# One core, decode step with adaLN, cached attention and a Mish MLP: the last weights loaded in another order and in more, smaller transfers, and four matmuls on zeros taken out

## The chip, the cores and the metric

One core of one Trainium2 chip. The metric is the device time of one execution in microseconds; the time of a kernel is the median of its runs. TensorE is PE in the profile (PEld is its weight load), VectorE is DVE, ScalarE is ACT, GpSimd is POOL, SyncE is SP. A letter q behind an engine (SPq) means its sequencer: it issues transfers and waits.

## The reference

Two rows (batch 2, one token each) of width 512 go through one transformer block. All inputs are float32.

```
mod = silu(c) @ w_mod, cut in six: sa, ca, ga, sb, cb, gb       # 512 wide each
h = layernorm(x) * (1 + ca) + sa
q = h @ wq                                # 32 heads of 128
p = softmax(q . k_cache * 128**-0.5)      # 4096 keys in each of 2 x 32 heads
x = x + ga * ((p @ v_cache) @ wo)
h = layernorm(x) * (1 + cb) + sb
a = h @ w1 + b1                           # 1376 wide
a = a * tanh(softplus(a))                 # Mish
out = x + gb * (a @ w2)
```

The two caches hold 268 MB of the 297 MB that are read. Everything else is weights: `w_mod`, `wq`, `wo`, `w1`, `w2`.

## The kernel before

Three rooms in SBUF, each of 64 KB a partition, take all large data in turn. In the first part a room holds the keys of one head and the values of an earlier head (`pair`); VectorE multiplies keys by the query and sums along the head (lines 336 and 340), ScalarE takes the exponentials, TensorE multiplies by the values (line 382). The list `plan` holds the loads in order with what each has to wait for: a load is issued as soon as everything that was in its room has been used (`used`, `holds`). All large loads are issued by one queue, SP's, from one line, 69, in the helper `load`. Transfers start in the order in which they are issued; an engine that needs a piece waits for the semaphore of the transfer that brings it.

After the last keys the rooms are filled once more, in this order: `wo` (all but its last two heads); `two`, the values of two heads, in two transfers; `last`, the values of the last head in two transfers (3072 and 1024 KB); the rest of `wo` (512 KB); `w1` in two transfers (1376 KB each); and `tail`. `tail` takes the room of `two`, so its transfers are issued when TensorE has used both heads of it (`values(H - 2)`, line 486). It holds the last sixth of `w_mod`, called `mod5` (1024 KB, 8 KB a partition), and `w2`, cut in 11 chunks of 128 rows and 512 columns (`NCH`, 256 KB each, 2 KB a partition). It arrives in four transfers: `mod5` with chunks 0 to 4 (2304 KB), chunks 5 to 7 (768 KB), chunks 8 and 9 (512 KB), chunk 10 (256 KB).

The work behind the last values is one chain: attention output (line 491), the second layernorm folded into the first layer (lines 502 to 559), Mish on VectorE and ScalarE (lines 572 to 580, its result is `actt`), and the second layer `yps` (line 585), 88 matmuls: eight records for each chunk, four groups of columns, two passes. Between the first layer and the second TensorE computes the gate `gb` from `mod5` (`modulation`, line 241, 32 matmuls; ScalarE copies it out by `keep`), then runs `idle(4)`: four matmuls of a tile of zeros, `busy`, into a PSUM bank that nobody reads any more (line 260). At the end VectorE multiplies `yps` by the gate (line 593), adds the residual (line 594), and SP issues the transfer of the output (line 595). Each engine runs its instructions in program order.

Of the kernel before, what the change touches and what calls it, by code (L numbers as in the profile page):

```python
# [7 lines left out]

F32 = mybir.dt.float32
BF16 = mybir.dt.bfloat16  # L10
AF = mybir.ActivationFunctionType
ALU = mybir.AluOpType
AX = mybir.AxisListType
# [1 line left out]
P = 128  # L15
# [3 lines left out]
D = 512  # L19
# [9 lines left out]
ROOM = 2 * KV  # L29
ALONE = (8, 16)  # L30
WO_FIRST = H - 2


def behind(h):
# [10 lines left out]
def kernel(ctx: ExitStack, tc: tile.TileContext, src: dict, out: bass.AP):  # L45
    nc = tc.nc
# [6 lines left out]
    const = ctx.enter_context(tc.tile_pool(name="const", bufs=1))  # L53
# [4 lines left out]
    def room(n, name):  # L58
        return rooms.tile([P, ROOM], F32, tag=f"room{n}", name=name)
# [7 lines left out]
    def load(t, lo, ap):  # L67
        piece = t[:, lo : lo + ap.shape[1]]
        nc.sync.dma_start(out=piece, in_=ap)
        return piece  # L70
# [26 lines left out]
    def load_wo(n):  # L97
        late["wo"] = room(n, "wo")
        load(late["wo"], 0, src["wo"][:, : WO_FIRST * D])
        w_t["wo"] = late["wo"].rearrange("p (h n) -> p h n", h=H)  # L100
# [6 lines left out]
    def load_last(n):  # L107
# [5 lines left out]
        lo = KV  # L113
        load(late["wo"], WO_FIRST * D, src["wo"][:, WO_FIRST * D :])
        w_t["w1"] = t[:, lo : lo + G * F].rearrange("p (k n) -> p k n", k=G)
# [7 lines left out]
    def load_tail(n):  # L123
# [4 lines left out]
        for part in src["w2"]:  # L128
            load(t, lo, part)
            lo += part.shape[1]  # L130


    plan, holds = [], {0: [("w", "wq")], 1: [("w", "mod")], 2: [("k", 0)]}
    order = (1, 0, 2)
    for h in range(1, H):
        n = order[(h - 1) % 3]
        plan.append((lambda n=n, h=h: load_keys(h, n), n, list(holds[n])))
        holds[n] = [("k", h)] + ([] if h in ALONE else [("v", behind(h))])
    n = order[(H - 1) % 3]
    for what, items in (  # L140
# [6 lines left out]
        n = order[(order.index(n) + 1) % 3]  # L147
    n = next(r for r in holds if holds[r] is not None)
# [3 lines left out]
    def used(*items):  # L152
# [8 lines left out]
    rows = ident.rearrange("p (g r) -> p g r", g=G)  # L161
# [6 lines left out]
        out=fold, in_=ident.rearrange("p (g r) -> p r g", g=G), axis=AX.X, op=ALU.add  # L168
# [3 lines left out]
        out=mean_w, in0=fold[:, None, :].to_broadcast([P, G, R]), scalar1=1.0 / D, scalar2=None, op0=ALU.mult  # L172
# [11 lines left out]
    ct = const.tile([P, G, R], F32, name="ct")  # L184
    ht = const.tile([P, G, R], F32, name="ht")
    h2t = const.tile([P, G, R], F32, name="h2t")
    x2t = const.tile([P, G, R], F32, name="x2t")
    e_t = [[const.tile([P, NB, R], F32, name=f"e{i}_{b}") for b in range(B)] for i in range(4)]
    ot_last = const.tile([P, 2 * B], F32, name="ot_last")
    busy = const.tile([P, 512], BF16, name="busy")  # L190
    for t in (ct, ht, h2t, x2t, *(t for pair in e_t for t in pair), busy):
        nc.gpsimd.memset(t, 0.0)
    ov = [psum.tile([P, 512], F32, tag=f"ov{i}", name=f"ov{i}", bufs=1) for i in range(2)]

# [41 lines left out]
    def modulation(name, lo, n, t):  # L236
        ps = wide_ps(f"modps{name}")[:, : n * P].rearrange("p (m n) -> p m n", m=n)
        t = t[:, :, D * lo : D * (lo + n)]
        for k in range(G):
            for g in range(G):  # L240
                nc.tensor.matmul(  # L241
                    ps[R * g : R * (g + 1)],
                    lhsT=ct[:, k, :],
                    rhs=t[:, k, :].rearrange("p (m n) -> p m n", m=n)[:, :, P * g : P * (g + 1)],
                    start=(k == 0),
                    stop=(k == G - 1),
                )
        return ps
# [5 lines left out]

    def small(name):
        return const.tile([P, G, B], F32, name=name)

    def idle(n):
        for _ in range(n):
            nc.tensor.matmul(ov[1], lhsT=busy[:, 0:P], rhs=busy, start=True, stop=True)  # L260


    cps = small_ps("cps")[:, : 2 * G * B]
# [39 lines left out]
    for half in range(2):  # L303
        ps = wide_ps(f"qps{half}")
        for k in range(G):
            for g in range(G):
# [3 lines left out]
                    lhsT=ht[:, k, :],  # L310
                    rhs=w_t["wq"][:, k, 512 * c : 512 * (c + 1)],
                    start=(k == 0),
                    stop=(k == G - 1),
# [148 lines left out]
    for g in range(G):  # L462
        nc.tensor.matmul(  # L463
            xps[:, g], lhsT=late["att_sb"][:, P * g : P * (g + 1)], rhs=fold[:, 0:B],
            start=(g == 0), stop=False, skip_group_check=True,
# [23 lines left out]
    for i in range(2):  # L489
        for g in range(G):  # L490
            nc.tensor.matmul(
                xps[:, g],
                lhsT=w_t["wo"][:, H - 2 + i, P * g : P * (g + 1)],
                rhs=ot_last[:, B * i : B * (i + 1)],
                start=False,
                stop=(i == 1 and g == G - 1),
# [31 lines left out]
    for k in range(1, G):  # L528
# [5 lines left out]
        out=st[:, 2], in0=v_sum, scalar1=-0.5 / D, scalar2=-0.5 * EPS, op0=ALU.mult, op1=ALU.add  # L534
# [17 lines left out]
    lo = 0  # L552
    for g in reversed(range(G)):
# [3 lines left out]
        lo = hi  # L557
    for j in range(NJ):
        nc.tensor.matmul(
            fps[:, G * B * j : G * B * (j + 1)],  # L560
            lhsT=hq_pad[:, P * j : P * (j + 1)],
            rhs=coef,
            start=False,
            stop=(j == NJ - 1),
            skip_group_check=True,
        )
    x2_rows = keep("x2", x2ps)
    gps = modulation("5", 0, 1, w_t["mod5"])
    idle(4)
    f = const.tile([P, 3, NJ * G, B], F32, name="f")  # L570
    hid = fps.rearrange("p (n b) -> p n b", b=B)
    nc.vector.tensor_scalar(out=f[:, 0], in0=hid, scalar1=30.0, scalar2=None, op0=ALU.min)
# [10 lines left out]
    for n in range(NCH):  # L583
        for t in range(G):
            nc.tensor.matmul(  # L585
                yps[R * t : R * (t + 1), :P],
                lhsT=actt[:, n, :],
                rhs=w_t["w2"][:, n, P * t : P * (t + 1)],
                start=(n == 0),
                stop=(n == NCH - 1),  # L590
# [5 lines left out]
        out=out.rearrange("b o (g n) -> g (b o) n", n=P),  # L596
        in_=y[0 :: R // B, :],
# [3 lines left out]
def _lay_out(np, a):  # L601
    def rows(w):
        return w.reshape(-1, P, w.shape[-1]).transpose(1, 0, 2)

    def eight(v):
        return v.reshape(B, G, P).transpose(1, 0, 2).reshape(G * B, P)

    def head_rows(t, h):
        return t[:, h].reshape(B, P, NS * DH).transpose(1, 0, 2).reshape(P, KV)

    def join(*parts):
        return np.ascontiguousarray(np.concatenate([t.reshape(P, -1) for t in parts], axis=1))

    k, v = a["A_k_cache"], a["A_v_cache"]
    pair = np.stack([join(head_rows(k, h), head_rows(v, o)) for h, o in PAIRS])
    single = np.stack(
        [head_rows(k, h) for h in (0, *ALONE)] + [head_rows(v, h) for h in (H - 3, H - 2, H - 1)]
    )
    wm = rows(a["w_mod"])
    starts = np.cumsum((0,) + WIDTHS)  # L620
    b1c = np.zeros((P, NJ * G, B), a["B_b1"].dtype)
    w2 = np.zeros((P, NCH, D), a["B_w2"].dtype)
    for n, (g, j) in enumerate(CHUNKS):
        f0 = starts[g] + P * j
        f1 = min(f0 + P, starts[g + 1])
        b1c[: f1 - f0, n] = a["B_b1"][f0:f1, None]
        w2[: f1 - f0, n] = a["B_w2"][f0:f1]
    return {
        "cx": np.ascontiguousarray(np.concatenate([eight(a["c"]), eight(a["A_x"])])),
        "mod01234": join(wm[:, :, : 5 * D], b1c),  # L630
        "wq": join(rows(a["A_wq"])),
        "pair": pair,
        "single": single,
        "wo": join(rows(a["A_wo"])),
        "w2_0": join(wm[:, :, 5 * D :], w2[:, :5]),
        "w1": join(rows(a["B_w1"])),
        "w2_1": join(w2[:, 5:8]),
        "w2_2": join(w2[:, 8:10]),
        "w2_3": join(w2[:, 10:]),
    }  # L640


# [18 lines left out]
```

## Time and profile before

| | us |
|---|---|
| median of 3 runs (698.69 to 698.79) | 698.79 |
| the profiled execution, device time | 698.93 |
| its span in the profile | 697.2 |
| DVE busy in the span | 587.6 |
| PE busy in the span | 292.9 |
| mean DMA rate over the span, GB/s | 427 |

In the span, time 0 is the start of the program on the core and all times are counted from it. The profiled execution lies 0.14 us above the median. What the change touches lies in the last 25 us, from the issue of `tail` at 672.9 us on. A row of a timeline has the start, the duration, the engine, the line, the operation and the tiles, and how long the engine was idle before it and who released it. A row on transfers has their number, the size of one and the time from issue to landing, which is the moment the last of the DMA engines that carry it has reported.

### The profile page before, as it was taken

Reading aid. Unit: us, or ns where it says so; the run is one execution under the profiler, and the core shown is the slowest. Engines: PE = TensorE matmul, PEld = TensorE weight load, DVE = VectorE, ACT = ScalarE, POOL = GpSimd, SP = SyncE. Lnnn points to the kernel's source line nnn. Section 1 sums busy time; section 2 is a strip of 40 time slices with the busy share of each in tenths; the row PEclk is TensorE's granted clock in tenths of the full one; section 3 lists DMA queues with packets and bytes.
Section 4 is the critical chain, followed back from the end, with each engine's and each line's share of the span. In section 5 each row is a group of like instructions: output and inputs, shape, how many; then the busy total and the mean of one; then the engine's idle time right before and its main releaser. Section 6 shows DMA issues by size and latency. Waiting matters only on the chain.

```text
span 697.2 us, 4054 instructions
## 1 busy us (share of the span) xinstructions
PE 292.9 (42%) x1679; PEld 100.6 (14%) x1680; DVE 587.6 (84%) x240; ACT 39.5 (6%) x187; POOL 4.7 (1%) x22
## 2 busy tenths in 40 slices
PE   2360435432350435443504453444322453443886
PEld 1110101110110101111101111111100111110244
DVE  3039999999899999999999999999999899999102
ACT  1000000000000000000000000000000000000000
POOL 2000000000000000000000000000000000000000
PEclk9775565666655666566655558665765566556879
DMA  9999999999999999999999999999999999999996
GB/s 407 406 448 425 432 456 429 422 429 440 445 429 425 426 440 440 432 430 416 446 440 430 432 432 437 432 429 440 429 433 432 426 440 432 433 432 413 434 418 252
DMA packets 6686, 297.49 MB, mean 427 GB/s; under 512 B 756, under 2 KB 780, under 8 KB 1292
## 3 DMA queue, kind: packets, MB, share of 16 engines
q1 hardware_dynamic: 6636, 297.23, 98.8%
q8 instruction: 13, 0.21, 0.1%
q14 instruction: 5, 0.04, 0.0%
q10 hardware_dynamic: 32, 0.01, 0.0%
HBM read 297.23 MB, written 0.00 MB: 426 GB/s over the span
## 4 chain that ended last, share of the span: by engine, by line
DMA 49%; DVE 45%; PE 5%; issue 0%; ACT 0%; SPq 0%; DVEq 0%
DMA kv<-in_pair 40%; DVE kv L336 22%; DVE s L340 21%; DMA two<-in_single 4%; PE ov L382 2%; DMA tail<-in_w 2%; DMA first<-in_mod 2%; PE modps L241 1%; DVE n L358 1%; DVE n L357 1%; PE yps L585 0%; PE otp L398 0%; PE att L422 0%; PE last_ps L463 0%; DVE m L350 0%
## 5 line engine op out<-in xcount | busy, mean ns | idle before, releaser
L336 DVE TENSOR_TENSOR kv<-kv,qb 128x8192 f32<-128x8192 f32 x32 | 277.9, 8684 | 44.2 <-DMA kv<-in_pair 22.5
L340 DVE TENSOR_REDUCE s<-kv 128x64 f32<-128x8192 f32 x32 | 277.4, 8667 | 0.0
L382 PE MATMUL ov<-kv,e 128*32 128x512 f32 x928 | 168.6, 893 | 5.2 <-ACT e L366 5.2
L362 PE MATMUL mb<-n,ones 2*128 2x2 f32 x64 | 17.7, 344 | 221.4 <-DVE n L358 221.4
L321 PE MATMUL qb<-q_sb,row_of 32*128 32x512 f32 x32 | 28.4, 1035 | 65.4 <-DVE kv L336 65.4
L382 PEld LDWEIGHTS ov<-kv,e 128*32 128x32 f32 x928 | 36.9, 156 | 118.7 <-issue 109.6
L362 PEld LDWEIGHTS mb<-n,ones 2*128 2x128 f32 x64 | 15.8, 303 | 230.3 <-issue 155.5
L352 PE MATMUL mt<-ident,m 128*2 128x128 f32 x64 | 13.7, 300 | 75.8 <-DVE m L350 75.8
L363 ACT COPY m<-mb 128x2 f32<-128x2 f32 x32 | 5.1, 160 | 532.2 <-PE mb L362 423.7
L366 ACT ACTIVATE e<-s,m 128x32 f32<-128x32 f32 x64 | 20.0, 314 | 1.2
L321 PEld LDWEIGHTS qb<-q_sb,row_of 32*128 32x128 f32 x32 | 8.8, 302 | 73.7 <-DVE kv L336 67.8
L352 PEld LDWEIGHTS mt<-ident,m 128*2 128x2 f32 x64 | 3.1, 82 | 97.4 <-DVE m L350 76.7
L410 DVE RECIPROCAL total<-l 128x8 f32<-128x8 f32 (+1 forms) x9 | 1.7, 184 | 14.7 <-PE l L408 14.7
L308 PE MATMUL qps<-wq,ht 128*32 128x512 f32 x64 | 9.5, 761 | 10.5 <-DMA wq<-in_wq 10.5
L366 ACT ACTIVATION_READ_ACCUMULATOR e<-s,m 128x1 f32 x64 | 11.9, 186 | 0.0
L398 PE MATMUL otp<-pick,o 128*128 128x8 f32 (+1 forms) x72 | 9.5, 258 | 3.9 <-ACT o L394 3.9
L382 PE MATMUL ov<-two,e 128*32 128x512 f32 x64 | 9.7, 763 | 0.3 <-DMA two<-in_single 0.3
L422 PE MATMUL att<-wo,ot 128*2 128x512 f32 x60 | 9.6, 742 | 0.4 <-DVE ot L401 0.3
L398 PEld LDWEIGHTS otp<-pick,o 128*128 128x128 f32 x72 | 8.7, 191 | 5.5 <-ACT o L394 5.5
L401 DVE TENSOR_TENSOR ot_last<-otp,total 128x4 f32<-128x4 f32 x1 | 0.2, 163 | 11.0 <-PE otp L398 11.0
L357 DVE TENSOR_REDUCE n<-mt 2x1 f32<-2x128 f32 x32 | 8.7, 272 | 0.5 <-PE mt L352 0.5
L394 ACT COPY o<-ov 128x512 f32<-128x512 f32 x9 | 5.3, 586 | 61.4 <-PE ov L382 61.4
(140 smaller groups left out, 107.2 us busy)
## 6 DMA issues: line engine op xcount, KB each, us to landing
kv<-in_single SPq DMA_DIRECT2D x3, 4096.0 KB, 31.1
two<-in_single SPq DMA_DIRECT2D x2, 4096.0 KB, 34.3
wo<-in_wo SPq DMA_DIRECT2D x1, 7680.0 KB, 39.1
first<-in_mod SPq DMA_DIRECT2D x1, 5132.0 KB, 15.1
last<-in_single SPq DMA_DIRECT2D x1, 3072.0 KB, 27.6
last<-in_w SPq DMA_DIRECT2D x2, 1376.0 KB, 34.7
tail<-in_w SPq DMA_DIRECT2D x1, 2304.0 KB, 16.2
last<-in_single SPq DMA_DIRECT2D x1, 1024.0 KB
```

The costliest lines, as they stand in the source:

```text
L241: nc.tensor.matmul(ps[R * g : R * (g + 1)], lhsT=ct[:, k, :], rhs=t[:, k, :].rearrange("p (m n) -> p m n", m=n)[:, :, P * g : P * (g + 1)] ...
L308: nc.tensor.matmul(ps[R * g : R * (g + 1)], lhsT=ht[:, k, :], rhs=w_t["wq"][:, k, 512 * c : 512 * (c + 1)], start=(k == 0), stop=(k == G - 1),
L321: nc.tensor.matmul(qb[:, b], lhsT=row_of[R * g : R * (g + 1), b], rhs=q_sb[R * g : R * (g + 1), half], start=True, stop=True,)
L336: nc.vector.tensor_tensor(out=k_t[h], in0=k_t[h], in1=qv, op=ALU.mult)
L340: nc.vector.tensor_reduce(out=s_t[h].rearrange("p b j -> p (b j)"), in_=k_t[h].rearrange("p b j d -> p (b j) d"), axis=AX.X, op=ALU.add,)
L352: nc.tensor.matmul(mps[h], lhsT=m_t[h][:, 0:2], rhs=ident, start=True, stop=True)
L357: nc.vector.tensor_reduce(out=n[:, 0:1], in_=mps[h], axis=AX.X, op=ALU.max, negate=True)
L362: nc.tensor.matmul(bps[:, 0:2], lhsT=ones[0:B, :], rhs=n[:, 1:3], start=True, stop=True)
L366: nc.scalar.activation(e_t[h % 4][b][:, :, lo : lo + 4], s_t[h][:, b].rearrange("p (c m) -> p c m", m=4), AF.Exp, bias=m[:, 2 + b : 3 + b] ...
L382: nc.tensor.matmul(ov[i % 2][R * g : R * (g + 1), :], lhsT=e_t[h % 4][b][:, c, :], rhs=v_t[h][:, b, 4 * c : 4 * c + 4, :].rearrange("p m d ...
L398: nc.tensor.matmul(tps[:, :n], lhsT=o[:, m, :], rhs=pick[:, m, at : at + n], start=(m == 0), stop=(m == 3))
L422: nc.tensor.matmul(att[R * g : R * g + B, :], lhsT=ot[:, B * h : B * (h + 1)], rhs=w_t["wo"][:, h, :], start=(h < G), stop=(h >= H - 2 - G),)
```

## The change

`tail` still takes the same bytes in the same room at the same places. What is cut, and how:

- `mod5` alone is the first transfer (1024 KB). Then chunks 0 to 5 (1536 KB), chunks 6 to 8 (768 KB), chunk 9 (256 KB).
- Chunk 10 comes in eight transfers by rows. The first has 16 rows (partitions), one for each of 16 DMA engines; the next have 28, 24, 20, 16, 12, 8 and 4 rows, two for each of 14, 12, 10, 8, 6, 4 and 2 engines (`ENDS`). The source is written as (engines, rows each, 512). So `tail` is twelve issues instead of four, all on SP's queue.
- `idle(4)`, its helper and the tile `busy` with its memset are gone.

```diff
+ENDS = ((16, 1),) + tuple((n, 2) for n in range(14, 0, -2))
+assert sum(n * each for n, each in ENDS) == P
...
         for part in src["w2"]:
             load(t, lo, part)
             lo += part.shape[1]
+
+        row = 0
+        for n, each in ENDS:
+            rows = slice(row, row + n * each)
+            nc.sync.dma_start(
+                out=t[rows, lo : lo + D], in_=src["w2_end"][rows].rearrange("(e r) n -> e r n", e=n)
+            )
+            row += n * each
...
-    busy = const.tile([P, 512], BF16, name="busy")
-    for t in (ct, ht, h2t, x2t, *(t for pair in e_t for t in pair), busy):
+    for t in (ct, ht, h2t, x2t, *(t for pair in e_t for t in pair)):
         nc.gpsimd.memset(t, 0.0)
...
-    def idle(n):
-        for _ in range(n):
-            nc.tensor.matmul(ov[1], lhsT=busy[:, 0:P], rhs=busy, start=True, stop=True)
...
     gps = modulation("5", 0, 1, w_t["mod5"])
-    idle(4)
...
-        "w2_0": join(wm[:, :, 5 * D :], w2[:, :5]),
+        "w2_0": join(wm[:, :, 5 * D :]),
         "w1": join(rows(a["B_w1"])),
-        "w2_1": join(w2[:, 5:8]),
-        "w2_2": join(w2[:, 8:10]),
-        "w2_3": join(w2[:, 10:]),
+        "w2_1": join(w2[:, :6]),
+        "w2_2": join(w2[:, 6:9]),
+        "w2_3": join(w2[:, 9:10]),
+        "w2_end": join(w2[:, 10:]),
```

More of the change, by code (lines that the diff above doesn't have):

```diff
@@ L9 @@
 F32 = mybir.dt.float32
-BF16 = mybir.dt.bfloat16
 AF = mybir.ActivationFunctionType
```

## The prediction

> **What bounds the kernel now.** I read the page first, for the chain that ended last, then that chain's last 25 us in order of time, then the transfers and SP's waits there.
>
> ```profile
> span 697.2 us, 4054 instructions
> DMA 49%; DVE 45%; PE 5%; issue 0%; ACT 0%; SPq 0%; DVEq 0%
> ...
> 666.82 6.08 PE ov L382 x32
> 672.91 0.02 issue
> 672.92 16.16 DMA tail<-in_w
> 689.09 0.14 issue
> 689.22 1.08 PE modps L241 x32
> 690.30 0.16 issue
> 690.46 0.81 PE ov L260 x3
> 691.27 2.58 PE yps L585 x88
> 693.86 0.03 issue
> 693.88 0.02 DVEq L593
> 693.90 0.04 issue
> 693.95 0.30 DVE y L593
> ```
>
> The last 25 us are two things. First a transfer: the 2304 KB of `tail` are issued at 672.92 and landed at 689.09. Then TensorE alone, without a pause: gate, idle matmuls, second layer. The three pieces of `w2` behind the first are on record too:
>
> ```profile
> tail<-in_w SPq DMA_DIRECT2D x1, 2304.0 KB, 16.2
> ...
> tail<-in_w SPq DMA_DIRECT2D x1, 768.0 KB, 17.6
> wo<-in_wo SPq DMA_DIRECT2D x1, 512.0 KB, 30.5
> tail<-in_w SPq DMA_DIRECT2D x1, 512.0 KB, 18.4
> ...
> tail<-in_w SPq DMA_DIRECT2D x1, 256.0 KB, 18.6
> ...
> 672.92 1.75 SPq L69 DMA_DIRECT2D tail<-in_w  x4
> ...
> 673.78 0.90 SPq L69 DMA_DIRECT2D tail<-in_w  x2
> ```
>
> Four issues in 1.75 us start at 672.9, 673.3, 673.8 and 674.2, so the pieces land at 689.1, 690.9, 692.2 and 692.8. Chunk 10 is there at 692.8, but its eight matmuls start only about 693.6 (691.2 plus 10/11 of 2.6 us). So the second layer is held by TensorE, 0.7 us behind the data. That is all that a better order can win, whatever happens elsewhere.
>
> How the transfers run out matters too:
>
> ```profile
> 689.10:690.90 1.80, 1.52 (x35) 1.15 (x36) 0.58 (x3) 0.27 (x1) 0.00 (x0) 1.00 0.55 220
> 690.90:692.20 1.30, 1.30 (x38) 1.00 (x40) 0.00 (x0) 0.00 (x0) 0.00 (x0) 1.00 0.25 91
> 692.20:692.90 0.70, 0.70 (x36) 0.70 (x32) 0.00 (x0) 0.00 (x0) 0.00 (x0) 1.00 0.02 6
> ```
>
> The last two columns are the busy share of the DMA engines and GB/s. With equal shares for all 16 they should end together; instead the share falls over 3.5 us to 0.25 and 0.02. Some engines are over 3 us ahead of others. Chunk 10 costs a late engine 692.8 - 692.2 = 0.65 us for 8 rows, 0.08 us a row.
>
> **The wait that I build on.** SP's own waits around `tail`, and the issue of the output:
>
> ```profile
> SPq L595 <- DVE y L594: 18.9, 1, 18.9
> ...
> SPq L595 <- DMA last<-in_single: 1.0, 1, 1.0
> SPq L657 <- DMA out<-y: 0.7, 1, 0.7
> ...
> L595 SPq EVENT_SEMAPHORE  x1: 17/17/17, 675.7 to 675.7; - x1
> ...
> 645.59 0.80 SPq L69 DMA_DIRECT2D last<-in_single  x2
> 646.44 0.43 SPq L69 DMA_DIRECT2D wo<-in_wo  x1
> 646.91 0.91 SPq L69 DMA_DIRECT2D last<-in_w  x2
> ```
>
> The issue of the output (line 595) waited twice: for `y`, which it needs, and 1.0 us, until 675.7, for the landing of a `last` transfer, with which it shares no byte. Count the issues: the second `last` piece, `wo`, twice `w1`, four of `tail`, output. The output is the eighth behind the transfer that it waited for. I read it as landing semaphores used in turn, eight of them: an issue waits until the transfer eight issues earlier has landed. Before, that costs nothing, because with four issues in `tail` the transfers eight back are old ones.
>
> **The change part by part.**
>
> The order of the first pieces. Up to 3584 KB the bytes before are the same, so landings follow by proportion. `w1` ends first:
>
> ```profile
> DMA to landing us min/median/max: 27.6/33.3/36.2
> ```
>
> This is the tile `last`; its longest belongs to the second half of `w1`, issued near 647.4, so it landed at 683.5. The 2304 KB then took 5.6 us. `mod5` alone (1024 KB) lands at 683.5 + 5.6 x 1024/2304 = 686.0; chunks 0 to 5 at 689.1 + 1.8 x 256/768 = 689.7; chunks 6 to 8 at 690.9 + 1.3/2 = 691.55; chunk 9 at 692.2.
>
> The gate and the idle matmuls. With `mod5` there at 686.0 the gate's 32 matmuls no longer wait for it. They can run when the first layer ends:
>
> ```profile
> 687.32 0.83 PE L559 MATMUL last_ps<-coef,last 128*128 128x8 f32 x6 [0.34 <-ACT last L556]
> ...
> 689.58 0.20 DVE L580 TENSOR_TENSOR last<-f 128x22 f32<-128x22 f32 x1
> ...
> 691.20 2.61 PE L585 MATMUL yps<-tail,last 128*32 128x128 f32 x88
> ```
>
> First layer done at 688.15, gate 1.08 us, done at 689.25, beside the Mish on VectorE, which ends at 689.78 as before. The second layer can start at 689.85 instead of 691.20: 1.08 us of gate and 0.81 us of idle matmuls leave the path, less the 0.5 us for which `actt` and chunks 0 to 5 are now late. It runs 48 matmuls at 2.61/88 = 0.030 us (1.4 us, to 691.3), then waits for 691.55, 24 more to 692.4, chunk 9 to 692.65. Chunk 10 ends it. The idle matmuls may also have kept the clock up; the three rows of windows above have 1.00 in the column before the DMA share. At half the clock the last eight matmuls would take 0.24 us more and their drain some 0.15; at the other end the cost is nothing. I take nothing, because the gate and 72 to 80 matmuls of the second layer fill most of 688.2 to 692.6. The memset of `busy` lies at the start on POOL, off the chain: nothing, at most its own fraction of a us in 700.
>
> The eight small transfers. Twelve issues at 0.43 us would be done by 678, long before the data of `w1` has passed, and cost nothing. But by the wait above each now waits for the transfer eight back: the one of 16 engines for `last` (675.7), that of 14 for `wo` (646.44 + 30.5 = 676.9), 12 and 10 for the halves of `w1` (until 683.5), 8 for `mod5` (686.0), 6 for chunks 0 to 5 (689.7), 4 for chunks 6 to 8 (691.55), and the last, on 2 engines, for chunk 9: it can't be issued before 692.2. SP's queue holds nothing else then but the output's issue, which comes later anyway; who waits is TensorE, for chunk 10.
>
> So the last transfer is issued at 692.2, or 692.25 if the issue before it (0.7 us, if as long as the output's) is still running. From issue to landing of so small a transfer on an empty queue there is one row, the output's:
>
> ```profile
> 694.60 0.70 SPq L595 DMA_DIRECT2D out<-y  x1
> ...
> 695.40:695.80 0.40, 0.00 (x0) 0.00 (x0) 0.00 (x0) 0.00 (x0) 0.00 (x0) 1.00 0.00 0
> 695.80:696.00 0.20, 0.00 (x0) 0.00 (x0) 0.00 (x0) 0.00 (x0) 0.00 (x0) 1.00 0.08 21
> ...
> L657 SPq DRAIN  x3: 7/7/7, 696.4 to 696.7; - x3
> ...
> cx<-in_cx ACTq DMA_DIRECT2D x1, 8.0 KB, 6.0
> ```
>
> Issued at 694.60, bytes move only after 695.8, and SP's wait for it has ended when its first drain stands at 696.4: 1.75 us. That is a store; a load of 8 KB took 6.0 us at the program's start, with 5 MB on the same engines. The engines are nearly empty here, so I stay near the lower end: 1.75 plus two rows (0.16) is about 1.95, with 1.75 to 2.6 for the range; the 6.0 stays outside. Landing: 694.2.
>
> From landing to line 593: 0.14 (as before the gate: landed 689.09, matmul 689.22), eight matmuls 0.24, the last one's own 0.27, 0.14 to VectorE, together 0.8; TensorE has eight semaphores to wait for before chunk 10, of which I allow 0.05 behind the last. Line 593 starts at 695.05 instead of 693.95. What follows is unchanged.
>
> **Sum.** +1.1 us: 1.35 won at the start of the second layer, all of it and 1.1 more lost at chunk 10. The profiled execution's 698.93 becomes 700.0; against the median, 0.14 lower, 699.9. That is 0.16% slower, and a difference within 0.2% (1.4 us) is about what a measurement of this kernel can't tell from no change.
>
> **The rivals.**
>
> *The issues are not held* (the 1.0 us wait of the output was something else). Then all twelve are queued by 678 and chunk 10 lands between 692.3 and 692.85, by how well the unequal shares meet the unequal engines. Line 593 then starts 0.8 us later, 693.2 at best behind chunk 9, 693.65 at worst: 0.3 to 0.75 us won, 698.3. For it: only one wait in the profile shows the rule clearly. Against it: that row has no other use.
>
> [...]
>
> *The split does nothing*: the wait is there, but chunk 10's last rows land by 693 all the same, since a small load is much quicker than the output's store. It would have to take 0.8 us; in the output's row no byte moved for 1.2 us. Time 698.8.
>
> **How the numbers follow.** Held issues as summed: 0.56, own range 699.5 to 700.5, a part of it above 700.2. Late engines or a landing at the long end, 700.2 to 701: 0.28. Not held: 0.10. Split does nothing: 0.06. The predicted time is 699.9; 698.9 to 700.9 leaves out the better part of the unheld case below and some of the long landings above. Faster by over 0.2% (below 697.4) needs more than the 0.75 us that there is: 0.02. Slower by over 0.2% (above 700.2): the second case and a little of the first, 0.33. Within: 0.65.
>
> **What would show it.** Right: the chain of waits ends with a `tail` transfer issued near 692.2, `yps` waits for it about 1.5 us, SP's waits name `tail` transfers, the gate stands at 688.2 with no wait for a transfer, line 593 starts near 695.0. Wrong: all twelve issues before 680, or the last ones with no wait of SP before them; then it is the first rival. [...] The prediction fails first if the eight-back rule is not one.

## The result, and the profile after

| | before | after |
|---|---|---|
| median of 20 runs, us | 699.0 | 700.17 |
| lowest, us | 698.69 | 699.79 |
| ratio to before, 95% interval | 1 | 1.0016 (1.0009 to 1.0023) |

The change makes the kernel 1.2 us, 0.16%, slower, and the interval does not reach 1. The first profile after is of an execution at 700.83 us, longer than most. The changed kernel was run again beside the experiments (`after_again`: median 700.17, 1.0013, 1.0004 to 1.0022), and that profile, of an execution at 700.24, is the one read from here on. The chain that ended last, in order of time (start, duration, what):

```profile
673.42 19.55 DMA tail<-in_w
692.97 0.02 issue
692.99 1.48 DMA tail<-in_w_end
694.47 0.24 issue
694.71 0.46 PE yps L588 x8
695.17 0.03 issue
695.20 0.02 DVEq L596
695.22 0.04 issue
695.26 0.30 DVE y L596
```

`in_w_end` is chunk 10, `in_w` the weights before it; an `issue` row is time in which the engine waited for nothing that the profile shows. Chunk 9, issued at 673.42, lands at 692.97. Only then is the last piece of chunk 10 issued, at 692.99; it lands at 694.47, and TensorE does the last eight matmuls alone. The multiplication by the gate (line 596, before 593) starts at 695.26 instead of 693.95. SP's own waits say why the piece was issued so late:

```profile
SPq L136 <- DMA tail<-in_w: 8.3, 4, 3.6
SPq L70 <- PE ov L386: 6.3, 1, 6.3
SPq L136 <- DMA last<-in_w: 5.9, 2, 3.0
SPq L598 <- DVE y L597: 2.6, 1, 2.6
SPq L136 <- DMA last<-in_single: 1.7, 1, 1.7
SPq L136 <- DMA wo<-in_wo: 0.9, 1, 0.9
```

Eight issues of line 136, eight waits: one for a `last` transfer, one for `wo`, two for `w1` (`last<-in_w`), four for the first four pieces of `tail`. That is the list of the transfers eight issues back, in full.

The second layer, in the same profile:

```profile
691.15 2.39 PE L588 MATMUL yps<-tail,last 128*32 128x128 f32 x80 [0.72 <-ACT mod L260]
694.68 0.19 PEld L588 LDWEIGHTS yps<-tail,last 128*32 128x32 f32 x8 [1.41 <-issue]
694.71 0.43 PE L588 MATMUL yps<-tail,last 128*32 128x128 f32 x8 [1.17 <-DMA tail<-in_w_end]
```

Eighty matmuls are done by 693.54, then TensorE stands 1.2 us, released by chunk 10. Before, the 88 ran without a pause.

And the running out of the transfers, microsecond by microsecond; the last two columns are the busy share of the DMA engines and GB/s. First before, then after:

```profile
689.00:690.00 1.00, 0.78 (x29) 0.81 (x32) 0.64 (x4) 0.00 (x0) 0.00 (x0) 1.00 0.69 274
690.00:691.00 1.00, 0.84 (x15) 0.34 (x7) 0.00 (x0) 0.27 (x1) 0.00 (x0) 1.00 0.40 158
```

```profile
689.00:690.00 1.00, 1.00 (x28) 0.98 (x31) 0.26 (x2) 0.22 (x1) 0.00 (x0) 1.00 0.69 209
690.00:691.00 1.00, 0.43 (x16) 0.16 (x8) 0.83 (x5) 0.27 (x1) 0.00 (x0) 1.00 0.60 186
```

In the first of them the engines are as busy as before (0.69) and move a quarter less (209 against 274 GB/s). Divide the rate by the share: before 397 and 395, after 303 and 310. A busy engine moves less. The prediction's sum had no such thing.

### The profile page after: what moved, and what is told of

Same layout as the page of the kernel before. It is cut to its first block, busy times and chain, and to the rows that moved or that the text cites. A ratio compares the mean times of both kernels' runs of the same rounds, so it can differ in the third digit from the quotient of the medians.

```text
span 699.1 us, 4058 instructions
## 1 busy us (share of the span) xinstructions
PE 292.2 (42%) x1676; PEld 100.5 (14%) x1676; DVE 587.0 (84%) x240; ACT 39.5 (6%) x187; POOL 4.3 (1%) x21
## 4 chain that ended last, share of the span: by engine, by line
DMA 49%; DVE 45%; PE 4%; issue 0%; SPq 0%; ACT 0%; DVEq 0%
DMA kv<-in_pair 40%; DVE kv L340 22%; DVE s L344 21%; DMA two<-in_single 4%; DMA tail<-in_w 3%; PE ov L386 2%; DMA first<-in_mod 2%; PE modps L249 1%; DVE n L362 1%; DVE n L361 1%; PE otp L402 0%; PE att L426 0%; PE last_ps L467 0%; DMA tail<-in_w_end 0%; DVE m L354 0%
## 5 line engine op out<-in xcount | busy, mean ns | idle before, releaser
L249 PE MATMUL modps<-first,ct 128*32 128x384 f32 (+1 forms) x64 | 6.7, 576 | 8.1 <-DMA first<-in_mod 8.1
```

Source lines behind the costliest of these rows:

```text
L249: nc.tensor.matmul(ps[R * g : R * (g + 1)], lhsT=ct[:, k, :], rhs=t[:, k, :].rearrange("p (m n) -> p m n", m=n)[:, :, P * g : P * (g + 1)] ...
```

## The experiments

All are timed in five rounds against the kernel before, whose median on the same chip was 698.87 beside whole, six, whole_held and whole_three and 698.86 beside all others.

| kernel | chunk 10 comes in | held by | median | ratio (95%) |
|---|---|---|---|---|
| whole | 1 transfer | nothing late | 698.63 | 0.9998 (0.9990 to 1.0007) |
| whole_three | 1, behind 3 small loads | w1, until 683.5 | 699.15 | 1.0001 (0.9993 to 1.0010) |
| whole_held | 1, behind 7 small loads | chunk 9 | 700.45 | 1.0023 (1.0014 to 1.0031) |
| six | 6, by rows | chunks 0 to 5 | 699.88 | 1.0015 (1.0007 to 1.0024) |
| six_again | the same | the same | 699.85 | 1.0011 (1.0002 to 1.0020) |
| after_again | 8, by rows | chunk 9 | 700.17 | 1.0013 (1.0004 to 1.0022) |
| four | 4, by rows, equal shares | w1, until 683.2 | 699.86 | 1.0012 (1.0004 to 1.0021) |
| columns | 4, by columns | w1, until 683.4 | 698.90 | 0.9998 (0.9989 to 1.0007) |
| rows96 | 1 of 96 rows | nothing late | 698.90 | 0.9998 (0.9989 to 1.0007) |
| rows96_8 | 1 of 96 rows, 8 engines | nothing late | 699.00 | 1.0003 (0.9995 to 1.0012) |
| before_noidle | before, no idle matmuls | | 698.70 | 1.0001 (0.9990 to 1.0012) |
| whole_idle | 1, idle matmuls back | nothing late | 698.88 | 1.0000 (0.9992 to 1.0009) |

**Everything but the small pieces (whole).**

```diff
-        row = 0
-        for n, each in ENDS:
...
+        load(t, lo, src["w2_end"])
```

> The changed kernel with chunk 10 as one transfer of 128 rows: five transfers in the tail instead of twelve, still no idle matmuls. Theory (the issues are held by the transfer eight back, and that decided the time): the fifth issue waits only for an old transfer, stands before 677, chunk 10 lands about 0.65 us behind chunk 9, where it landed before, and line 593's multiplication starts 0.8 us later; against the kernel before 0.3 us faster, against the changed kernel 1.3 us faster. Rival (the missing idle matmuls or the order of the pieces cost the time): stays near the changed kernel, 1 us slower than before.

```profile
675.36 17.23 DMA tail<-in_w_end
692.58 0.04 issue
692.63 0.47 PE yps L582 x8
693.10 0.03 issue
693.12 0.02 DVEq L590
693.14 0.04 issue
693.19 0.30 DVE y L590
```

Issued at 675.36, landed at 692.58: the last eight matmuls still wait for chunk 10, and line 590 starts 0.6 us behind its landing. In this profile line 590 (before 593) starts 0.76 us earlier than before; in the medians 0.24 us are left, which the interval does not tell from nothing. Against the changed kernel it is about 1.5 us faster. So `mod5` alone, the other cuts and the missing idle matmuls do not cost the time; the eight pieces do.

**The hold by itself (whole_held, whole_three).** Seven loads of 8 KB that nobody needs put chunk 10 eight issues behind chunk 9; three do not.

```diff
...
+        for i in range(7):
+            nc.sync.dma_start(out=t[:16, lo + D + P * i : lo + D + P * (i + 1)], in_=src["cx"])
         load(t, lo, src["w2_end"])
```

> As the kernel with chunk 10 whole, with seven loads of 8 KB into unused columns of the room between chunk 9 and chunk 10, so that chunk 10 is the eighth issue behind chunk 9. Theory: SP waits for chunk 9 to land, then issues chunk 10; that lands about 2.1 us later (1.6 as the last transfer of the changed kernel, plus 7 more rows an engine at 0.08), 1.5 us later than without the seven; 1.1 us slower than before. Rival (no such rule; issues are only queued): as the kernel with chunk 10 whole, within 0.2 us.

> As the kernel with chunk 10 whole, with three such loads of 8 KB instead of seven, so that chunk 10 is the eighth issue behind the second half of w1, landed near 683.5. Theory of the eight: no cost that shows (0.1 us), as the kernel with chunk 10 whole; 1.4 us faster than with seven. Rival (each small extra transfer costs by itself): three sevenths of the cost of seven, about 0.6 us.

The chain of the kernel with seven, and of its transfers the row of chunk 10:

```profile
673.56 18.55 DMA tail<-in_w
692.12 0.02 issue
692.13 2.61 DMA tail<-in_w_end
694.74 0.04 issue
...
695.35 0.30 DVE y L592
...
tail<-in_w_end SPq DMA_DIRECT2D x1, 256.0 KB, 2.6
```

Chunk 9 lands at 692.12, chunk 10 is issued at 692.13. The time is 1.8 us longer than with chunk 10 whole (expected 1.5). The profile with three is of an execution 3 us above its kernel's median, with TensorE's granted clock at 0.50 from 679 to 689, so only its landings are read: chunk 10 landed 9.5 us after an issue at 683.53, at 693.05, 0.8 us behind chunk 9 instead of the 0.65 of whole. By the medians the three cost 0.5 us, which the intervals do not tell from 0; the 1.3 us between three and seven lie outside them. That an issue waits for the landing of the transfer eight issues back is shown (692.12 and 692.13); that a small extra transfer costs nothing is not.

**The pieces without the late hold (six, six_again).**

```diff
-ENDS = ((16, 1),) + tuple((n, 2) for n in range(14, 0, -2))
+ENDS = ((16, 1), (14, 2), (12, 2), (10, 2), (8, 2), (12, 2))
```

> Chunk 10 in six transfers: the first five as in the changed kernel (16, 28, 24, 20, 16 rows), then 24 rows in one instead of 12, 8 and 4 in three. The sixth is the tenth transfer of the tail and waits for chunks 0 to 5, not for chunk 9. Theory of held issues: issued near 690.3, landed with the slow engines' other rows near 694.4 in the time of the changed kernel's profile, 0.6 us before its 695.05; so 0.6 us faster than the changed kernel, 0.5 us slower than before. Rival (small transfers by rows are slow by themselves, held or not): no faster than the changed kernel.

```profile
672.69 17.00 DMA tail<-in_w
689.68 0.02 issue
689.70 3.94 DMA tail<-in_w_end
693.65 0.24 issue
693.89 0.46 PE yps L588 x8
...
694.44 0.30 DVE y L596
...
tail<-in_w SPq DMA_DIRECT2D x1, 256.0 KB, 19.1
```

The sixth piece is issued at 689.70 (expected near 690.3), when chunks 0 to 5 have landed, and lands at 693.65, 0.8 us before the last of the changed kernel. But the kernel is still 1.0 us slower than before, not 0.5: chunk 9 itself (issued at 673.6, 19.1 us) lands at 692.7, where it landed at 691.9 with chunk 10 whole. The direct comparison was run once more on one chip:

> The changed kernel once more, beside the kernel with chunk 10 in six transfers, on one chip. Both write chunk 10 in small pieces into other engines' partitions; only here is the last piece held by chunk 9. Theory (the hold sets the end): the last transfer stands at the landing of chunk 9, lands 1.6 us behind it, and the kernel is 0.4 to 0.7 us slower than the one with six. Rival (the meeting of engines sets the end and the hold hides behind it): equal within 0.2 us.

> Chunk 10 in six transfers, the last one held by chunks 0 to 5 only, on one chip with the changed kernel. If the hold sets the end of the changed kernel: 0.4 to 0.7 us faster than that. If the meeting of engines does: equal within 0.2 us; in both cases about 1 us slower than before, since chunk 9 lands 0.7 us later than with chunk 10 whole.

700.17 against 699.85: 0.3 us for the hold, less than the 0.4 to 0.7 of the one theory and more than the 0.2 of the other, with overlapping intervals; and `six` also deals out its last 24 rows in another way. That the hold stands last in the changed kernel is shown by its chain; that removing it alone brings back more than 0.3 us is not. The larger part, 1.0 us, is there without it.

**Why small pieces by rows are slow (four, columns).** Four transfers each, equal shares for all engines, none held late. One cuts by rows, the other by columns.

```diff
-ENDS = ((16, 1),) + tuple((n, 2) for n in range(14, 0, -2))
+ENDS = ((16, 2),) * 4
```

```diff
...
+        for at in range(0, D, P):
+            load(t, lo + at, src["w2_end"][:, at : at + P])
```

> Chunk 10 in four transfers of 32 rows, two rows for each of 16 engines: equal shares as in one transfer of 128 rows, none of the four held by a late transfer, but each engine writes other partitions than its usual ones. Theory (engines that are ahead write where the late engines write, and both slow down, while the sum of bytes for one entry of SBUF stays): packets of 6 KB on the late engines take about 0.3 instead of 0.24 us, chunk 9 lands 0.3 to 0.6 us later than with chunk 10 whole, and chunk 10 at most 0.2 later. First rival (the slowing is lost time): chunk 10 lands 0.6 us or more later. Second rival (no meeting of engines): as with chunk 10 whole.

> Chunk 10 in four transfers of 128 rows and 128 columns (512 bytes a row) instead of four of 32 rows and 512 columns. Equal shares, small pieces, none held by a late transfer, but all 128 partitions in each, so that every engine keeps the partitions that it has in all large transfers. Theory (pieces by rows are slow because engines meet in one another's partitions): packets of 6 KB stay at 0.237 us, chunk 9 lands as with chunk 10 whole, and the time is that of chunk 10 whole within 0.3 us (four times the packets, of 512 bytes). Rival (small transfers slow the others, whatever they write): chunk 9 0.7 us later, 1 us slower, as with four of 32 rows.

Chunk 9, chunk 10 and the two microseconds from 689 to 691, first by rows, then by columns:

```profile
tail<-in_w SPq DMA_DIRECT2D x1, 256.0 KB, 19.8
...
683.24 10.22 DMA tail<-in_w_end
693.47 0.25 issue
...
689.00:690.00 1.00, 0.94 (x32) 0.67 (x27) 0.64 (x5) 0.22 (x1) 0.00 (x0) 1.00 0.76 236
690.00:691.00 1.00, 0.34 (x13) 0.37 (x17) 0.46 (x3) 0.27 (x1) 0.00 (x0) 1.00 0.60 219
```

```profile
tail<-in_w SPq DMA_DIRECT2D x1, 256.0 KB, 19.1
...
689.00:690.00 1.00, 1.00 (x33) 0.79 (x32) 0.56 (x4) 0.22 (x1) 0.00 (x0) 1.00 0.78 283
690.00:691.00 1.00, 0.28 (x13) 0.26 (x13) 0.57 (x3) 0.27 (x1) 0.00 (x0) 1.00 0.51 175
```

By rows chunk 9 was issued at 672.9 and landed 19.8 us later, at 692.7, and chunk 10 at 693.47: 0.7 and 0.9 us later than whole. By columns chunk 9 was issued at 673.0 and landed at 692.1, chunk 10 at 692.85, and the time is that of the kernel before (698.90). GB/s over busy share is 311 by rows and 363 by columns in the first microsecond, but 365 and 343 in the next: this ratio alone does not tell the two apart. The packets do. Those of 6 KB (chunks 6 to 8; before, chunks 5 to 7) took 237 ns on average before, whole and by columns (246 at most), 260 by rows with 436 at most, and 262 with 411 at most in the changed kernel.

The landings in all traces agree. From the landing of the second half of `w1` to that of chunk 9 the same bytes arrive in every kernel, `mod5` and chunks 0 to 9. This took 8.65 to 8.75 us in every kernel that brings chunk 10 in 128 rows (before, whole, columns, whole_three, whole_held and the two on idle matmuls), and 9.14 to 9.60 us in every one that brings it in transfers of fewer rows. The 9.14 are those of rows96, below, where chunk 10 is a single transfer. It is the late engines that lose: the first engine reported chunk 9 at 688.67 in whole and at 688.56 in the changed kernel, the last at 691.94 and at 692.97.

So it is not the number or the size of the pieces; it is the cut by rows. Why is not shown. The meeting of engines in one another's partitions, on which the expectations build, is my guess: the packets on record name neither engine nor partition, so no row shows that an engine has usual partitions or that two engines meet in one. The rows of the source change along with the partitions, and no run tells reading from writing.

My theory of `four` fell in one point: I had taken the sum of bytes for one place as fixed, which no run shows, and expected chunk 10 at most 0.2 us later. It landed 0.9 us later. With equal shares a late engine has no fewer rows of its own, so the 0.7 us that chunk 9 landed later come on top.

**Fewer rows (rows96, rows96_8).** The 32 rows of zeros in chunk 10 are neither loaded nor multiplied; in the second kernel a gap in the source after every 12 rows leaves the transfer to 8 engines. Of the second kernel's edit:

```diff
...
-        "w2_end": join(w2[:, 10:]),
+        "w2_end": np.pad(w2[: P - R, 10].reshape(8, 12, D), ((0, 0), (0, 1), (0, 0))),
```

> Chunk 10 as one transfer of 96 rows (the other 32 hold zeros and are neither loaded nor multiplied) on 16 engines, 6 rows each instead of 8, in other partitions than the engines' usual ones. By bytes alone 0.16 us faster than with chunk 10 whole. By the meeting of engines: packets of 6 KB go up to 0.3 us while the early engines write their 6 rows, chunk 9 lands 0.3 to 0.5 us later, and the kernel is 0.2 to 0.5 us slower than with chunk 10 whole.

> Chunk 10 holds 96 rows of weights and 32 rows of zeros; here only the 96 are loaded and multiplied, in one transfer whose source has a gap after every 12 rows, so that 8 engines carry it, 12 rows each; five transfers in the tail, no idle matmuls. If the late engines are not among the 8 lowest-numbered: their share of chunk 10 is gone, and only writes into their partitions by others remain; chunk 10 lands with chunk 9, line 593 starts 0.3 to 0.6 us earlier than with chunk 10 whole, 0.6 to 0.9 us faster than before. Rival (the late ones are among them): 12 rows at 0.08 to 0.16 us behind chunk 9, 0.3 to 1.3 us slower than with chunk 10 whole.

96 rows: chunk 9 at 692.5 instead of 691.9, then a shorter chunk 10 (192 KB) at 692.9 instead of 692.6; the 6 KB packets took 261 ns with 478 at most. In its profile the second layer ran without a pause, so these landings did not set the end. The median, 698.90, is 0.27 us above whole, where the meeting of engines had given 0.2 to 0.5 slower and the bytes alone 0.16 faster; the intervals do not tell 0.27 from nothing. 8 engines: the transfer reported from eight engines, seven of which had landed by 692.0 and the eighth at 693.54, 0.9 us behind chunk 9: 12 rows at 0.077. The median is 0.4 us above whole, at the low end of what the rival of this expectation gave (0.3 to 1.3); the intervals overlap. From 692.65 on one engine in sixteen works:

```profile
692.65:693.05 0.40, 0.40 (x20) 0.19 (x8) 0.00 (x0) 0.00 (x0) 0.00 (x0) 1.00 0.06 20
```

One of the eight that this transfer uses is a late one. The changed kernel's ramp gives most rows to the engines that it uses most often, which helps only if all of these are early. Whether they are the ones that this transfer uses, no row says.

**The idle matmuls (before_noidle, whole_idle).**

> The kernel before without its four idle matmuls, nothing else. Theory: the second layer starts at 690.35 instead of 691.2 and runs into the landing of chunk 10 at 692.85; line 593 starts 0.3 us earlier, 0.3 us faster. Rival (they keep the clock up): the granted clock in the second layer falls below 1.00 and the 88 matmuls take longer, 0.3 us or more slower.

> The changed kernel with chunk 10 as one transfer, and with the four idle matmuls back behind the gate. Theory: they run in 689.3 to 690.1, while the second layer waits for its data anyway; same as without them within 0.1 us. Rival (clock): faster than without them by 0.3 us.

Neither taking them out of the kernel before (698.70 against 698.86) nor putting them back (698.88 against 698.63 for whole) makes a difference that the intervals show; 0.3 us faster had been expected of the first. The granted clock in the second layer was 1.00 without them, in whole from 690 on and after in the rows further up; in before_noidle the 88 matmuls took 2.64 us, with the idle matmuls 2.58 (before).

## Why the prediction was right, and where it was not

The forecast was 699.9, 1.1 us and 0.16% slower, in a range of 698.9 to 700.9; measured 700.17, 1.17 us above before. The place and the mechanism of the last wait are as forecast; the size is right by luck, since two of its terms were off in opposite ways, and in the changed kernel the held issue is worth only some 0.3 us, by the comparison with `six`. The forecast took a difference within 0.2% for about what a measurement can't tell from no change; 20 runs told 0.16%.

- **The eight-back wait**: right. It rested on one row, the output's 1.0 us wait for a `last` transfer. After, SP's eight waits name the eight transfers that the prediction lists, and whole_held makes the same wait in another kernel. The landing records of the traces show it directly: SP's transfers behind the last keys report to eight semaphores one after the other, and the ninth to the first again.
- **Landings by proportion**: the step that failed. "Up to 3584 KB the bytes before are the same, so landings follow by proportion" gave 692.2 for chunk 9; it landed at 692.97. The bytes were the same, but with chunk 10 cut by rows the late engines' packets took longer, which the sum had at nothing. That term measured 0.8 us against the forecast; between the profiles of whole and of four, six and after_again it is 0.7, 0.8 and 1.0.
- **Issue to landing of the last piece**: 1.95 taken, 1.48 measured (1.58 in the first profile). Under the lower end of my bounds, 1.75, which came from a store.
- **Landing to line 593**: 0.85 taken, 0.79 measured (695.26 - 694.47); 0.61 where chunk 10 comes in one transfer. It is 0.79 with four and with six pieces too, so a chunk 10 in pieces costs about 0.2 here, not more with more pieces; the forecast allowed 0.05.
- Together: 0.77 more, 0.47 less, 0.06 less and 0.03 less for the issue, 695.26 instead of 695.05.
- **The gate and the idle matmuls**: the gate no longer waited for its weights, and the idle matmuls were worth nothing. The start of the second layer moved between profiles (689.56 in whole, 691.15 here) and decided nothing here.
- **The first rival**, issues not held, gave 698.3. Cut by rows and not held late it is 699.9 (six, four); whole and not held it is 698.63. The rival counted 0.3 to 0.75 us of gain and missed that the pieces cost 1.0 without a late hold. So the sign of the result does not hang on the hold, as the prediction had it: either alone makes the kernel slower, the cut by rows (four) or the hold (whole_held).
- **Late engines** (0.28 for 700.2 to 701, together with a landing at the long end): there are late ones, by 4.4 us between the first report of chunk 9 and the last (688.56 and 692.97). But the last piece landed 1.48 us after its issue, and in rows96_8, where one late engine is left alone, its 12 rows took 0.077 us each, no more than the 0.08 that I had taken. What got slower lies ahead of chunk 10: the 6 KB packets of chunks 6 to 8 took 260 ns on average and up to 436 by rows (four), 237 and 246 at most by columns. What in the chip makes them slower no row names.
- **The split is not what the source says.** The prediction took two engines for the last piece. Its packets, in the first profile after:

```profile
DMA packets 8, 0.01 MB, mean 10 GB/s; under 512 B 4, under 2 KB 4, under 8 KB 8
```

Four rows and four reports: four engines, a row each. The pieces of 16, 12, 8 and 4 rows went out on 16, 12, 8 and 4 engines, not 8, 6, 4 and 2; those of 28, 24 and 20 rows on 14, 12 and 10, as written. I read it so that source rows that lie one behind the other are one run, however they are written; that is my reading of these counts alone. With a gap in the source (rows96_8, 12 rows for each of eight engines) the cut holds: eight reports.

No version here beats the kernel before by more than the measurement can tell; whole is the fastest by its median, 698.63.

## What to carry to other kernels

Count the transfers on a queue before cutting one into more: with the eight landing semaphores that are used in turn here, an issue waits for the landing of the one eight issues back, and a piece added at the end of a stream is held by the stream's own last pieces. Cut the last piece of a stream by columns, or not at all: here every cut by partitions slowed the late engines on pieces that were already on their way (from the landing of `w1` to that of chunk 9 it took 9.14 us and more, by columns 8.75 at most). A forecast can be right in its number with two terms wrong; compare each landing, not only the sum.

## What the runs showed of the hardware that was not expected

- Transfers cut by rows slow packets of other transfers that run beside them: 6 KB packets of 237 ns went up to 411 to 478 ns, and from 689 to 690 the rate over the busy share fell by a quarter (397 to 303 GB/s).
- A single load of 8 KB on engines that are nearly empty took 1.5 to 1.6 us from issue to landing, less than the 1.75 of the output's store.
- TensorE's stretch at half clock did not end at the same time in each profile. In that of before the granted clock was back at 1.00 from 685.4; in that of whole_three it was still 0.50 up to 689; in that of after_again it was 0.50 until 688, and the second layer could start only at 691.15:

```profile
686.00:688.00 2.00, 2.00 (x19) 1.17 (x13) 0.00 (x0) 0.00 (x0) 0.00 (x0) 0.50 0.98 408
```
